# A decode block on one Trainium2 core: W_gate loaded in three pieces by partitions, x in three loads instead of five

## The chip, the core and the metric

The kernel runs on one core of a Trainium2 chip. A core has a matrix engine (TensorE, PE), a vector engine (VectorE, DVE), a scalar engine (ScalarE, ACT), GpSimd (POOL), a queue engine that only issues and waits (SyncE, SP), and sixteen DMA engines that bring data from the device's memory into the 128 partitions of the on-chip memory. The metric is the device time of one execution in microseconds (us); lower is better. A load here means one DMA instruction; a load over 128 partitions is cut into rows, one to a partition, and the rows are dealt out to the DMA engines.

## What is computed

One decode step of a transformer layer for two sequences (B = 2, one new token each): layer norm, attention over a cache of 8192 positions with 32 heads of 128, a residual, a second layer norm, and a gated feed-forward with a rectified gate.

```python
# x (2,1,512); k_cache, v_cache (2,32,8192,128); wq (512,4096); wo (4096,512)
# W_gate, W_up (512,1376); W_down (1376,512); all bfloat16
q = layernorm(x) @ wq                      # 32 heads of 128
p = softmax(q . k_cache * 128 ** -0.5)
h = x + (p . v_cache) @ wo
n = layernorm(h)
gate = n @ W_gate
gate = gate * (gate > 0)
out = h + (gate * (n @ W_up)) @ W_down
```

The two caches are 268 MB of the 281 MB that are read, so the work is mostly a stream of cache tiles through the core.

## The kernel before

All of the order is written by hand: the body stands under `tc.manual_schedule()`, and each engine executes its instructions in the order of the text.

The on-chip memory holds three large buffers, `bufs[0]` to `bufs[2]`, of 64 KB in each partition. A tile of K or V covers four heads of one sequence (8 MB) and fills one buffer. A "step" is one such group of heads: 15 full steps and, for the last four heads, two half steps of two heads each (`steps`, `Q` is the last full step). K of step i lies in buffer 2i mod 3 and V in 2i+1 mod 3, so that one of the three is always being filled. Within a step VectorE multiplies the K tile by the query (L375) and adds up along the head dimension (L393, L395), while TensorE and ScalarE take a share of the positions by transposing them (L349, L350, L340). Then come the softmax's exponentials (L415) and the product with V on TensorE (L446).

The loads are issued by two queues. ScalarE's queue issues only x: five loads at L190, into `xr`, two rows of `bufs[2]`. SP's queue issues everything else, in the order of the text: W_q (L193), K and V of the first step (L165, `load_tile`), then one cache tile each time a buffer comes free, and in the last stage W_o in six pieces (L567, L589, L590), W_gate and W_up (L612), three pieces of the last 96 rows of W_down (L616) and four loads with the rest of it (L621). A load waits on its issuing queue until the buffer that it writes has been read. The tile framework numbers the loads of both queues round eight semaphores, so that a load also waits until the load eight before it has landed.

At the front TensorE transposes x (L238), VectorE and ScalarE norm it (`ln_cols`, L172 to L185), TensorE multiplies it with W_q (L252), and the queries are spread over the partitions (L259 to L276). This work needs x and W_q, and runs while the first K tile is still on its way. At the end the attention output is multiplied by W_o (`attend_set`, `attend`), normed, and goes through W_gate and W_up (`through`, L686) and W_down (`down`, L719). W_gate and W_up lie behind each other in `bufs[2]` as `wgu`: partition p holds rows 4p to 4p+3 of the matrix, 11,008 bytes for each of the two. The copies at L734 and L735 and the store at L736 close the kernel.

Of the kernel before, what the change touches and what calls it, by code (L numbers as in the profile page):

```python
# [13 lines left out]
def _free(t, offset, dims):  # L14

    return bass.AP(tensor=t.tensor, offset=t.offset + offset, ap=[t.ap[0]] + [list(d) for d in dims])


def _dram(t, offset, dims):
    return bass.AP(tensor=t.tensor, offset=t.offset + offset, ap=[list(d) for d in dims])  # L20
# [3 lines left out]
def kernel(  # L24
# [13 lines left out]
    nc = tc.nc  # L38
    P = nc.NUM_PARTITIONS
# [3 lines left out]
    F = B_W_gate.shape[1]  # L43
    KC = D // P
# [81 lines left out]
    wgu = bufs[2][:, HALF:HALF + 2 * KC * F].rearrange("p (k c f) -> p k c f", k=2, c=KC)  # L126
# [59 lines left out]

    with tc.manual_schedule():

        for b, k, n in ((0, 0, 2), (0, 2, 2), (1, 0, 2), (1, 2, 1), (1, 3, 1)):
            nc.scalar.dma_start(  # L190
                out=xr[b:b + 1, k * P:(k + n) * P], in_=_dram(A_x, b * D + k * P, [[D, 1], [1, n * P]]),
            )
# [9 lines left out]
            out=nscale, in_=nscale, compare_op=ALU.not_equal, fill=-SCALE,  # L202
# [5 lines left out]
            out=ident_f, in_=ident_f, compare_op=ALU.not_equal, fill=1.0,  # L208
# [4 lines left out]
            out=sel, in_=sel, compare_op=ALU.not_equal, fill=1.0,  # L213
# [9 lines left out]
            out=pick, in_=pick, compare_op=ALU.not_equal, fill=1.0,  # L223
# [24 lines left out]
        for g0 in range(0, NQ, 4):  # L248
            for n0 in range(NH * g0 * Dh, NH * (g0 + 4) * Dh, 4 * Dh):
                q_ps = ps2.tile([B, 4 * Dh], f32, tag="o")  # L250
                for c in range(KC):
                    nc.tensor.matmul(  # L252
                        out=q_ps, lhsT=xn[:, c, :], rhs=wq_sb[:, c, n0:n0 + 4 * Dh], start=(c == 0), stop=(c == KC - 1),
                    )
                nc.vector.tensor_copy(qrow[:, n0:n0 + 4 * Dh], q_ps)
            for b in range(B):
                r_ps = ps2.tile([P, 4, Dh], f32, tag="tp")
                for j in range(NH):
                    nc.tensor.matmul(  # L259
                        out=r_ps[j * (P // NH):(j + 1) * (P // NH)], lhsT=sel[:, b, 0:P // NH],  # L260
# [5 lines left out]
        for j in range(2):  # L266
            nc.tensor.matmul(
                out=r_ps[j * (P // 2):(j + 1) * (P // 2)], lhsT=sel[:, B - 1, :],
# [102 lines left out]
        def products(s, t0=0, t1=None):  # L371

            n = (s.nv if t1 is None else t1) - t0
            kv = _free(s.kt, t0 * Dh, [[Dh, n], [1, Dh]])
            nc.vector.tensor_tensor(out=kv, in0=kv, in1=_free(s.qr, 0, [[0, n], [1, Dh]]), op=ALU.mult)  # L375
# [211 lines left out]
        for k in range(1, len(SETS)):  # L587
# [3 lines left out]
            out=wo[:, (HM + 1) * D:Hq * D], in_=_dram(A_wo, (HM + 1) * Dh * D, [[P // 4 * D, 4], [D, P // 4], [1, D]]),  # L591
# [16 lines left out]
        scores_pe(p1, lambda: next(turns)())  # L608
        act_sums(p1)
        products(p1, 48)  # L610
        for w, src in ((0, B_W_gate), (1, B_W_up)):
            nc.sync.dma_start(  # L612
                out=wgu[:, w].rearrange("p c f -> p (c f)"), in_=_dram(src, 0, [[KC * F, P], [1, KC * F]]),
            )
        for q0 in range(AGAIN, P, AGAIN):
            nc.sync.dma_start(  # L616
                out=wd_sb[q0:q0 + AGAIN, FC - 1, :], in_=_dram(B_W_down, (F - P + q0) * D, [[D, AGAIN], [1, D]]),
            )
        for f0, n in FSETS[:-1]:
# [10 lines left out]
            out=z2_ps, lhsT=ones, rhs=_free(zc, ((B - 1) * NQ + groups[Q][1]) * NH, [[1, nb]]), start=True, stop=True,  # L630
# [63 lines left out]
        for c in range(KC):  # L694
            nc.tensor.transpose(hT_ps[:, c, :], hb[:, c].rearrange("p k b -> p (k b)"), ident)
        nc.scalar.activation(
            out=hrow.rearrange("q (p c) -> q p c", c=KC), in_=hT_ps.rearrange("q c p -> q p c"), func=ACT.Copy,
# [9 lines left out]
            out=gate, in0=g_ps, scalar=0.0, in1=_free(rvar, 0, [[0, FC], [1, B]]), op0=ALU.max, op1=ALU.mult,  # L707
# [16 lines left out]
        for t, (part, _, _) in zip(u_ps, parts):  # L724
            through(t, 1, part)
            f = slice(part[0], part[-1] + 1)
# [40 lines left out]
```

## Time and profile before

| | us |
|---|---|
| median of 3 runs | 659.67 (659.04 to 659.94) |
| profiled execution | 659.39 |
| its span in the profile | 657.5 |
| VectorE busy | 558.1 (85% of the span) |
| TensorE busy (matmul) | 352.1 (54%) |
| ScalarE busy | 123.6 (19%) |
| bytes read | 281.05 MB, 427 GB/s over the span |

"Busy" is the time in which an engine executes; the span runs from the first to the last event of the profile, and what the profiled execution took beyond it lies before and after the span. The page divides the span into 40 slices and gives for each engine the busy share in tenths (9 is 90% or more). The chain of waits is followed back from the last instruction: at each step to whatever released it. In its lines, and in those of the timeline, the columns are the start in us, the duration in us, and what it was; a name such as `tile L375` is the written tile and the line in the program, and SPq and ACTq are queue instructions, such as the issue of a load. A line of the waits reads: engine, line, what was waited for, then the total in us, the number of waits and the longest. A load's time in the chain is from its issue to its last completion, with the time that it stands behind earlier loads in it. For each load the trace also records the completions, one for each DMA engine that took part, and every single packet with its start, its duration and its size.

### The profile page before, as it was taken

The numbers are of one execution on the slowest core, as the hardware profiler recorded it, in microseconds if no ns is written. First come the engines' busy times: TensorE is split into PE (matmuls) and PEld (weight loads), VectorE is DVE, ScalarE is ACT, GpSimd is POOL, SyncE is SP. The second block draws the span as 40 slices with busy tenths as digits, with TensorE's granted clock in tenths as the row PEclk, the third lists the DMA queues.
The fourth block names the chain that finished last, engine by engine and source line by source line (L and its number), as shares of the span: only waits on it lengthen the run. The fifth ranks groups of instructions, "written<-read, shape, count | busy, mean of one in ns | idle before, by whom it ended". The sixth has DMA issues, their size and how long they took to land.

```text
span 657.5 us, 5117 instructions
## 1 busy us (share of the span) xinstructions
PE 352.1 (54%) x2118; PEld 158.9 (24%) x2118; DVE 558.1 (85%) x252; ACT 123.6 (19%) x337; POOL 24.1 (4%) x36
## 2 busy tenths in 40 slices
PE   0730934809175380926539092552918458291997
PEld 0310311304022130312204031220403224030456
DVE  0599697988979799897979989796997969999982
ACT  0230030200203020030301103030210304201870
POOL 3080000000000000000000000000000000000020
PEclk9975775958778596877959687695968869686895
DMA  9999999999999999999999999999999999999997
GB/s 383 447 444 447 387 440 443 447 399 444 439 443 436 419 436 435 439 439 436 423 443 424 439 440 427 447 416 443 439 423 440 423 443 436 423 444 413 425 425 291
DMA packets 6948, 281.37 MB, mean 428 GB/s; under 512 B 809, under 2 KB 1422, under 8 KB 1934
## 3 DMA queue, kind: packets, MB, share of 16 engines
q1 hardware_dynamic: 6916, 281.06, 99.1%
q8 instruction: 16, 0.26, 0.1%
q14 instruction: 6, 0.05, 0.0%
q10 hardware_dynamic: 10, 0.00, 0.0%
HBM read 281.05 MB, written 0.00 MB: 427 GB/s over the span
## 4 chain that ended last, share of the span: by engine, by line
DVE 42%; DMA 37%; PE 18%; ACT 1%; issue 1%; ACTq 0%; SPq 0%; DVEq 0%
DMA tile<-in_A_k_cache_dram 30%; DVE tile L375 19%; DVE tile L393 18%; PE pv_ps L446 16%; DMA tile<-in_A_wo_dram 4%; DVE scol L395 2%; DMA tile<-in_A_x_dram 2%; DMA tile<-in_B_W_down_dram 1%; PE q_ps L252 1%; DVE pgq L420 1%; ACT ecol L415 1%; DVE pm L399 1%; DVE qrep L395 0%; DVE pm L410 0%; DVE hmax L412 0%
## 5 line engine op out<-in xcount | busy, mean ns | idle before, releaser
L446 PE MATMUL pv_ps<-tile,pgq 128*16 128x512 bf16 x960 | 244.3, 421 | 235.8 <-DVE pgq L420 223.2
L375 DVE TENSOR_TENSOR tile<-tile,qrep 128x29696 bf16<-128x29696 bf16 (+3 forms) x16 | 232.4, 14524 | 44.9 <-DMA tile<-in_A_k_cache_dram 44.9
L393 DVE TENSOR_TENSOR tile<-tile 128x14848 bf16<-128x14848 bf16 (+7 forms) x68 | 236.4, 3477 | 2.2
L446 PEld LDWEIGHTS <-pgq 128*16 128x16 bf16 x960 | 91.6, 97 | 378.1 <-DVE pgq L420 234.5
L451 ACT ACTIVATE pv<-pv_ps 16x512 f32<-16x512 f32 (+1 forms) x16 | 9.4, 589 | 243.7 <-PE pv_ps L446 243.6
L350 ACT ACTIVATE tile<-t_ps 128x1024 bf16<-128x1024 bf16 x53 | 52.6, 1022 | 12.6 <-PE t_ps L349 12.1
L415 ACT ACTIVATE ecol<-scol,nmax 128x256 bf16<-128x256 f32 x14 | 7.1, 508 | 196.1 <-DVE nmax L414 196.1
L340 PE MATMUL row_ps<-tile,qz 128*24 128x512 bf16 (+1 forms) x98 | 30.1, 389 | 18.0 <-ACT tile L350 17.9
L349 PE MATMUL t_ps<-ident,tile 128*128 128x128 bf16 x424 | 32.3, 229 | 13.0 <-DMA tile<-in_A_k_cache_dram 13.0
L349 PEld LDWEIGHTS <-tile 128*128 128x128 bf16 x424 | 25.8, 103 | 28.1 <-issue 14.2
L395 DVE TENSOR_REDUCE scol<-tile 128x232 f32<-128x1856 bf16 (+1 forms) x14 | 28.9, 2067 | 0.5
L641 POOL TENSOR_TENSOR tile<-ident 6x2 bf16<-6x2 bf16 x1 | 2.1, 2147 | 583.5 <-ACT tile L381 583.5
L420 DVE TENSOR_TENSOR pgq<-ecol,ownb 128x1024 bf16<-128x1024 bf16 x15 | 10.4, 692 | 10.3 <-ACT ecol L415 10.3
L381 ACT ACTIVATE tile<-tile 128x128 bf16<-128x128 bf16 x60 | 17.6, 293 | 1.9 <-DVE tile L375 1.9
L281 POOL COPY qzp<-qTs 128x4 bf16<-128x4 bf16 x1 | 15.0, 14982 | 26.1 <-DVE qTs L276 26.1
L375 DVE TENSOR_TENSOR tile<-tile,qpair 128x4096 bf16<-128x4096 bf16 (+3 forms) x4 | 15.5, 3883 | 0.0
L340 PEld LDWEIGHTS <-qz 128*24 128x24 bf16 (+1 forms) x98 | 7.9, 92 | 27.6 <-issue 22.7
L239 DVE CAST xc<-x_ps 128x8 f32<-128x8 bf16 x1 | 0.2, 167 | 15.5 <-PE x_ps L238 15.5
L367 ACT ACTIVATE scol<-sc_ps 32x24 f32<-32x24 f32 (+1 forms) x56 | 11.7, 209 | 7.7 <-PE sc_ps L362 7.2
L362 PE MATMUL sc_ps<-ident_f,tile 24*128 24x24 f32 (+2 forms) x68 | 7.2, 220 | 11.1 <-ACT tile L358 11.1
L358 ACT ACTIVATE tile<-row_ps 24x512 f32<-24x512 f32 (+2 forms) x17 | 10.0, 586 | 13.5 <-PE row_ps L340 13.5
L381 ACT ACTIVATION_READ_ACCUMULATOR tile<-tile 128x1 f32 x60 | 11.2, 186 | 0.0
(133 smaller groups left out, 143.8 us busy)
## 6 DMA issues: line engine op xcount, KB each, us to landing
tile<-in_A_k_cache_dram SPq DMA_DIRECT2D x2, 4096.0 KB
tile<-in_A_v_cache_dram SPq DMA_DIRECT2D x2, 4096.0 KB, 19.6
tile<-in_A_wq_dram SPq DMA_DIRECT2D x1, 4096.0 KB, 12.2
tile<-in_A_wo_dram SPq DMA_DIRECT2D x1, 2048.0 KB
tile<-in_B_W_gate_dram SPq DMA_DIRECT2D x1, 1376.0 KB, 22.8
tile<-in_B_W_up_dram SPq DMA_DIRECT2D x1, 1376.0 KB
tile<-in_A_wo_dram SPq DMA_DIRECT2D x1, 1024.0 KB, 23.8
tile<-in_B_W_down_dram SPq DMA_DIRECT2D x1, 640.0 KB
```

Source lines behind the costliest of these rows:

```text
L281: nc.gpsimd.tensor_copy(qzp[:, :, 6:8], qTs[:, B - 1, Hq - NH:Hq].rearrange("p (k j) -> p k j", j=2),)
L340: nc.tensor.matmul(out=row_ps, lhsT=z, rhs=s.kt[:, (nv + c0 + k) * Dh:(nv + c0 + k + 4) * Dh], start=(u == 0), stop=(u == U - 1),)
L349: nc.tensor.transpose(t_ps[:, k, :], s.kt[:, t * Dh:(t + 1) * Dh], ident)
L350: nc.scalar.activation(out=s.kt[:, (nv + c0) * Dh:(nv + c0 + TPC) * Dh], in_=t_ps.rearrange("p t s -> p (t s)"), func=ACT.Copy,)
L367: nc.scalar.activation(out=scols[s.i][r, nv:s.nt].rearrange("p (u t) -> p t u", t=4), in_=sc_ps[r, :, :, j], func=ACT.Copy,)
L375: nc.vector.tensor_tensor(out=kv, in0=kv, in1=_free(s.qr, 0, [[0, n], [1, Dh]]), op=ALU.mult)
L381: nc.scalar.activation(out=kv, in_=kv, func=ACT.Copy, accum_out=scols[s.i][:, t:t + 1])
L393: nc.vector.tensor_tensor(out=lo, in0=lo, in1=hi, op=ALU.add)
L395: nc.vector.tensor_reduce(out=scol[:, s.na:s.nv], in_=_free(s.kt, s.na * Dh, [[Dh, s.nv - s.na], [1, 8]]), axis=AXIS.X, op=ALU.add,)
L415: nc.scalar.activation(out=ecol, in_=scols[s.i], func=ACT.Exp, scale=SCALE, bias=nmax, accum_out=zs[:, s.b, s.g:s.g + 1],)
L420: nc.vector.tensor_tensor(out=s.pg, in0=_free(ecol, 0, [[VG, s.nt // VG], [0, NH], [1, VG]]), in1=_free(ownb, 0, [[0, s.nt // VG], [VG, NH ...
L446: nc.tensor.matmul(out=pv_ps[s.i][r, :], lhsT=s.pg[:, u].rearrange("p j t -> p (j t)"), rhs=s.vt[:, u * VG * Dh:(u + 1) * VG * Dh], start= ...
```

## The change

x comes by three loads: the first sequence's 512 values by one, the second's by two of 256. W_gate, before one load over 128 partitions, comes by three, over partitions 0 to 7, 8 to 15 and 16 to 127; W_up stays one load. The number of loads in the whole program stays the same (two fewer on ScalarE's queue, two more on SP's).

```diff
-        for b, k, n in ((0, 0, 2), (0, 2, 2), (1, 0, 2), (1, 2, 1), (1, 3, 1)):
+        for b, k, n in ((0, 0, 4), (1, 0, 2), (1, 2, 2)):
             nc.scalar.dma_start(
                 out=xr[b:b + 1, k * P:(k + n) * P], in_=_dram(A_x, b * D + k * P, [[D, 1], [1, n * P]]),
             )
...
-        for w, src in ((0, B_W_gate), (1, B_W_up)):
-            nc.sync.dma_start(
-                out=wgu[:, w].rearrange("p c f -> p (c f)"), in_=_dram(src, 0, [[KC * F, P], [1, KC * F]]),
-            )
+        for w, src, cuts in ((0, B_W_gate, (0, 8, 16, P)), (1, B_W_up, (0, P))):
+            for q0, q1 in zip(cuts, cuts[1:]):
+                nc.sync.dma_start(
+                    out=wgu[q0:q1, w].rearrange("p c f -> p (c f)"),
+                    in_=_dram(src, q0 * KC * F, [[KC * F, q1 - q0], [1, KC * F]]),
+                )
```

## The prediction

> **What bounds the kernel now.** First the page: its second part (the span in 40 slices) and its fourth (the chain that ended last).
>
> ```profile
> span 657.5 us, 5117 instructions
> ...
> DVE  0599697988979799897979989796997969999982
> DMA  9999999999999999999999999999999999999997
> ...
> HBM read 281.05 MB, written 0.00 MB: 427 GB/s over the span
> ```
>
> The DMA row has no gap in it until the last slice; VectorE, the busiest engine, has. The span is the time that 281 MB take. The trace keeps every DMA packet, and I followed the sixteen DMA engines packet by packet: from 1.8 us until 654 us each packet starts within some nanoseconds of the end of the one before it on its engine. A change pays only if it shortens or rebalances what those sixteen carry.
>
> Second, the chain in order of time, at its two ends:
>
> ```profile
> 2.11 12.96 DMA tile<-in_A_x_dram
> 15.07 0.14 issue
> 15.20 0.28 PE x_ps L238 x4
> ...
> 30.63 0.31 PE r_ps L267 x2
> 30.96 41.50 DMA tile<-in_A_k_cache_dram
> 72.48 15.64 DVE tile L375
> ...
> 618.99 24.67 DMA tile<-in_A_wo_dram
> ...
> 644.18 9.77 DMA tile<-in_B_W_down_dram
> 653.94 0.04 issue
> 653.99 0.60 PE d_ps L719 x15
> 654.61 0.33 PE d_ps L719 x4
> 654.97 0.27 ACT tile L735
> ```
>
> At the front x lands at 15.07, and the second K tile's load is issued at 30.96. Its 41.50 us are not its own: an 8 MB load takes 19.3 us, so it stood behind two others. At the back W_down's last pieces land at 653.94 and, by the landing records, 654.57; four matmuls, the copies and the store follow: 2.9 us of tail. The profiled execution took 659.39 us: 657.5 of span and 1.9 around it. The median of the runs, 659.67, is 0.28 more, and I add that to every time below.
>
> Third, the waits of SP's queue, which issues all loads but x:
>
> ```profile
> SPq L616 <- DMA tile<-in_A_v_cache_dram: 9.3, 1, 9.3
> SPq L612 <- DMA tile<-in_A_wo_dram: 4.5, 1, 4.5
> SPq L612 <- DMA tile<-in_A_v_cache_dram: 4.4, 1, 4.4
> SPq L621 <- DMA tile<-in_B_W_gate_dram: 2.6, 1, 2.6
> ```
>
> A load waits until the one issued eight loads before it has landed (there are eight load semaphores, taken in turn): L612 for V's half tile, L621 for W_gate.
>
> The landing records also show what no page prints: the sixteen engines don't finish together. Each load has sixteen completions, and W_gate's are (us):
>
> ```
> 644.59 644.62 644.65 644.65 644.77 645.14 646.10 646.12
> 646.35 646.36 647.37 647.48 647.54 647.58 647.59 647.63
> ```
>
> Six engines are done by 645.1, six only from 647.4 on. The lead grows over the run by steps of about 1.6 us, each on one engine, just after one of sixteen 16 KB packets of the instruction queue (q8, at 36.8, 94.8, 155.4 us and so on, 0.88 to 1.0 us each); they go round eight engines, twice. W_down's last load ends at 651.57 on the first engine and 654.57 on the last: the slow engines set the end.
>
> **The change, part by part.**
>
> *x.* Its completions are at 1.96, 7.74, 10.19, 12.62 and 15.07 us: after the first, each load costs one turn between W_q's packets for its data and one for its semaphore, 2.44 us. With three the last lands at 10.19, 4.88 us earlier, whatever the bytes (512 or 1,024 B are one packet of some 25 ns). The queries follow, 3.5 us from x to the normed row, at 13.7; W_q's last completion, 12.96, is just ahead. What hides the 4.88 us is the K tile behind it: K's first tile completes at 32.26, and VectorE's first product starts at 32.41. So at most 0.15 us there, and then nothing: the K load issued at 30.96 could be issued at 26 and would still stand behind V, which lands at 53.1. Were that cover gone, x would be worth up to 4.88. I take 0.
>
> *W_gate, how it is spread.* The engines that a load uses show in its completions: one row of x, one; the two rows of the output, two; 32 rows of W_down, sixteen, with two rows each in the packets; 128 rows, sixteen with eight. I take eight rows as eight engines with one row each, and 112 as sixteen with seven. Of 128 rows, eight engines then carry nine and eight carry seven, where each had eight. A row of 11,008 B takes 413 ns in the packets. So eight engines end 0.41 us later than before and eight 0.41 earlier. The sum has two ends: -0.41 if all slow engines are among the relieved, +0.41 if one slow engine is among the loaded; the packets do not name their engine, and I could follow the engine that carries x only up to a three-way tie at 92.4 us. One slow engine among the loaded is enough, so I take +0.41.
>
> [...]
>
> *W_gate, how it is issued.* SP issues two loads more, 0.33 us each, in time in which it waits anyway. By the eight-loads rule W_gate's three pieces wait for V's half tile (624.8), for the first part of W_o (629.7, where W_up was issued) and for V's last half tile (639.3). W_up now waits for the second part of W_o, 641.8; W_down's pieces queue behind it: 643.1, 643.7, 644.0, 644.3, then each W_gate piece in turn, the last at about 648 instead of 647.6. Do the engines run dry? The earliest engine finishes W_o at 641.32. The piece issued at 639.3 needs some 1.0 us to its first packet (W_q: issued at 0.74, first packet at 1.78), so 1.0 us is left. W_up, issued at 641.8, arrives at 642.9 and is needed at 644.2 (641.32 and seven rows). W_down's last piece is needed at 651.3. No gap: 0. The matmuls that read W_gate start at 648.24, waiting for VectorE; W_gate now lands at about 648.0, still ahead.
>
> *Sum:* 0 + 0.41 + 0 = +0.41: 659.39 + 0.41 = 659.80, and with 0.28 660.1 us.
>
> **The rivals.**
>
> *Eight adjacent rows share a way into memory (slower).* The place is the two eight-row loads: eight engines write eight neighbouring partitions at once. If these can take no more than one or two engines' pace, the rows queue. Between none and all eight in series (8 x 0.413 = 3.30 us instead of 0.41) lie 0 and 2.9 us a load, 0 and 5.8 for both, on top of the 0.41. For it: no load of the trace has put so many bytes into so few partitions. Against it: the rows of the 32-row loads, two to an engine, take 46 ns per 1,024 B, exactly as in the 128-row loads; but those are too short to fill anything. Halfway, 2.9 us: 659.39 + 0.41 + 2.9 + 0.28 = 663.0 us. It decides from 0.9 us for the pair on a slow engine; if the eight are the six early ones and two more, their 3 us lead hides most of it.
>
> [...]
>
> *x was the bound after all (faster).* The chain does run through x, and VectorE's first product starts 0.15 us after K's tile. Up to 4.88 us: 654.8. Against it: the DMA engines have no gap between 1.8 and 654 us, and their bytes stay.
>
> *It does not do what it says.* If an eight-row load were cut over all sixteen engines, nothing moves but x: 659.7.
>
> **How the numbers follow.** The forecast (every row at its engine's own pace, one row more or less per engine) has 0.43, the shared way 0.41, x 0.10, no effect 0.06. The forecast's own range is 659.1 to 660.4: -0.41 to +0.41 around 659.67 with some scatter (the runs lie 0.9 us apart). A difference under 0.2%, 1.3 us, is about what a measurement of this kernel can tell from no change. Within it lie the forecast and no effect: 0.49. Slower by more is the shared way: 0.41; faster is x: 0.10. The range reaches from 659.0 to the shared way's 663.0; outside are x and the upper part of the shared way, together some 0.2.
>
> **What would show it.** x's last completion near 10.2 us and VectorE's first product still at 32.3 to 32.4: x is hidden. The 11,008 B packets: eight engines with nine, eight with seven. If those packets stay at 413 ns and W_down's last completion lies within 0.5 us of 654.57, the forecast's price is right; if the packets of the first two loads are stretched to two or four times 413 ns, the shared way is there. W_down's completions should lie closer together if the loaded engines are the early ones, and wider apart if they are the late ones. The prediction is wrong if the end moves by more than 1.3 us, or if a gap opens on an engine between 640 and 650 us because a load was issued too late.

## The result and the profile after

| | us |
|---|---|
| median after, 6 runs | 664.89 (664.13 to 665.96) |
| median before beside it, 6 runs | 659.53 (659.04 to 659.94) |
| ratio | 1.0083 [1.007, 1.0096] |
| profiled execution after, its span | 665.37, 663.6 |

The change makes the kernel 5.4 us slower, and the span of the profiled execution is 6.1 us longer. The page of the changed kernel, in the same lines as before:

```profile
span 663.6 us, 5115 instructions
...
DMA  9999999999999999999999999999999999999996
GB/s 379 442 439 442 442 436 403 431 443 432 443 438 436 411 436 438 431 435 436 438 427 432 438 443 419 435 439 435 431 435 436 423 436 438 438 406 437 438 349 196
...
HBM read 281.05 MB, written 0.00 MB: 424 GB/s over the span
```

The bytes are the same, and the DMA row still has no gap until the last slice. What is new stands in the GB/s row, last slice but one: 349 after 438 in the slice ahead of it. The engines are as busy there as ever and bring less. The same row of the kernel before has no such drop, 425 in both slices:

```profile
GB/s 383 447 444 447 387 440 443 447 399 444 439 443 436 419 436 435 439 439 436 423 443 424 439 440 427 447 416 443 439 423 440 423 443 436 423 444 413 425 425 291
```

The chain of waits after (start, duration, what), at its two ends, and then its last pieces:

```profile
1.53 8.68 DMA tile<-in_A_x_dram
13.70 5.84 PE q_ps L252 x16
...
26.71 45.49 DMA tile<-in_A_k_cache_dram
72.31 15.64 DVE tile L375
...
624.99 22.45 DMA tile<-in_B_W_gate_dram
647.49 12.51 DMA tile<-in_B_W_down_dram
```

```profile
660.04 0.59 PE d_ps L721 x10
...
660.67 0.33 PE d_ps L721 x4
```

x has landed at 10.21 us (1.53 + 8.68), and the matmuls of the queries run from 13.70. The second K tile's load is issued at 26.71, 4.25 us earlier than before, but now takes 45.49 us instead of 41.50: both end at about 72.2 to 72.5, and VectorE's second step begins at 72.31 where it was 72.48. V's first half tile lands at 624.92 (before: 624.77) and its last half tile at 639.41 (before: 639.28). So all but 0.1 us of the loss lies after 639 us. W_down's last completion is at 660.63; it was 654.57.

The next view divides the last stage into stretches. Its columns: from and to, length, the busy time (and count) of PE, PEld, VectorE, ScalarE and POOL, then the granted clock of TensorE, the DMA engines' busy share and GB/s. Before:

```profile
642.00:646.00 4.00, 3.68 (x109) 3.59 (x108) 0.78 (x5) 0.00 (x0) 0.00 (x0) 0.50 1.04 432
646.00:650.00 4.00, 3.23 (x77) 3.07 (x75) 1.33 (x9) 0.00 (x0) 0.00 (x0) 0.50 1.00 401
650.00:654.00 4.00, 3.61 (x82) 2.97 (x83) 1.02 (x6) 0.59 (x1) 0.00 (x0) 0.50 0.70 267
```

After:

```profile
642.00:646.00 4.00, 3.65 (x108) 3.56 (x107) 0.80 (x5) 0.00 (x0) 0.00 (x0) 0.50 1.12 250
646.00:650.00 4.00, 1.70 (x32) 1.46 (x29) 1.33 (x9) 0.00 (x0) 0.00 (x0) 0.50 1.01 224
650.00:654.00 4.00, 0.00 (x0) 0.03 (x1) 0.00 (x0) 0.00 (x0) 0.00 (x0) 0.50 0.93 265
```

The share in the last column but one is near 1 in both; the last column falls from 432 and 401 to 250 and 224 GB/s. The packets say how: the 11,008 B packets, one row of W_gate or W_up each, took 413 ns before (median; mean 419.5) and take 729 ns after (mean 695, longest 1,082). Their sum grew from 107.4 to 177.9 us, 70.5 us over sixteen engines or 4.4 us for each. Packets of other loads that are in flight at the same time are stretched too: 31 of W_o's last 128 packets of 4,096 B take up to 324 ns instead of 159. The sixteen completions of W_down's last load come 5.2 us later in the mean; the last of them, 1.3 us behind that mean before, is now 2.2 us behind it, which makes up the 6.1 us. PE pays for it: from 646 to 650 us it is busy for 1.70 us instead of 3.23.

SP's waits after:

```profile
SPq L613 <- DMA tile<-in_A_v_cache_dram: 14.1, 2, 9.4
...
SPq L623 <- DMA tile<-in_B_W_gate_dram: 5.8, 2, 5.6
SPq L618 <- DMA tile<-in_A_wo_dram: 2.8, 3, 2.0
```

W_down's last load waits 5.6 us (before: 2.6) for W_gate's third piece, whose last completion is at 653.87. This is a consequence and not the cause: no engine falls idle for it, since sixteen packets or more are under way at every full microsecond from 640 to 656.

### The profile page after: what moved, and what is told of

Read it like the earlier page. It is cut to its first block, busy times and chain, and to the rows that moved or that the text cites. A ratio compares the mean times of both kernels' runs of the same rounds, so it can differ in the third digit from the quotient of the medians.

```text
span 663.6 us, 5115 instructions
## 1 busy us (share of the span) xinstructions
PE 353.8 (53%) x2118; PEld 159.7 (24%) x2118; DVE 558.2 (84%) x252; ACT 123.7 (19%) x337; POOL 9.1 (1%) x36
## 4 chain that ended last, share of the span: by engine, by line
DVE 42%; DMA 40%; PE 17%; ACT 1%; issue 1%; ACTq 0%; DVEq 0%; SPq 0%
DMA tile<-in_A_k_cache_dram 30%; DVE tile L375 19%; DVE tile L393 18%; PE pv_ps L446 15%; DMA tile<-in_B_W_gate_dram 3%; DMA tile<-in_A_v_cache_dram 3%; DVE scol L395 2%; DMA tile<-in_B_W_down_dram 2%; PE q_ps L252 1%; DMA tile<-in_A_x_dram 1%; DVE pgq L420 1%; ACT ecol L415 1%; DVE pm L399 0%; DVE qrep L395 0%; DVE pm L410 0%
## 5 line engine op out<-in xcount | busy, mean ns | idle before, releaser
L362 PEld LDWEIGHTS sc_ps<-ident_f,tile 24*128 24x128 f32 (+2 forms) x68 | 5.5, 136 | 19.4 <-ACT tile L358 19.4
L252 PE MATMUL q_ps<-tile,xn 128*2 128x512 bf16 x32 | 9.5, 460 | 1.0 <-DVE xn L185 1.0
```

What stands on the lines that cost most here:

```text
L252: nc.tensor.matmul(out=q_ps, lhsT=xn[:, c, :], rhs=wq_sb[:, c, n0:n0 + 4 * Dh], start=(c == 0), stop=(c == KC - 1),)
L362: nc.tensor.transpose(sc_ps[:, t].rearrange("p u j -> p (u j)"), rows[:, t * P:(t + 1) * P], ident_f[0:nh * U, 0:nh * U],)
```

## The experiments

Each kernel was timed beside the kernel before on the same chip; ratios are to that, with 95% intervals. All of them have x in three loads, so that only the last stage differs between them. The diffs are against the changed kernel where its line with the cuts stands with a minus, against the experiment before in one section that says so, and otherwise against the kernel before, without the part on x; `...` marks lines left out. "Packets" are those of 11,008 B.

### x alone

```diff
-        for w, src, cuts in ((0, B_W_gate, (0, 8, 16, P)), (1, B_W_up, (0, P))):
+        for w, src in ((0, B_W_gate), (1, B_W_up)):
...
```

> x in three loads, W_gate in one as before. Every theory that puts the loss into W_gate's pieces expects the time of the kernel before, 659.5 us within 0.5, with x's last completion at 10.2 us and VectorE's first product still at 32.3 to 32.4. Were x to blame in part, the time would lie between 659.5 and 664.9.

659.47 us, ratio 1.0004 [0.9995, 1.0013]; packets 413 ns; span 657.5 us, as before. x costs and gives nothing.

### The eight-row loads alone

W_gate stays one load; two loads of eight rows are added, into partitions 0 to 7 and 8 to 15 of a part of `bufs[2]` that is not read.

```diff
+        for q0 in (0, 8):
+            nc.sync.dma_start(
+                out=bufs[2][q0:q0 + 8, HALF + 2 * KC * F:TILE],
+                in_=_dram(B_W_gate, q0 * KC * F, [[KC * F, 8], [1, TILE - HALF - 2 * KC * F]]),
+            )
```

> W_gate in one load of 128 partitions, and ahead of it two loads of eight partitions (10,752 B a row) into unused memory: the eight-row loads alone, at the cost of 16 rows more to read. Theory A (the load of 112 partitions is what halves the pace: its rows, seven to an engine, take the engines off the ways into memory that they have to themselves) expects only the extra bytes: two rows on eight engines, 0.8 us at most, 659.5 to 660.4. Theory B (the rows of an eight-row load queue behind each other in a few partitions, as in the rival of the prediction) expects most of the loss: 662 to 666 us, with row packets stretched well over 413 ns around the two loads only.

661.12 us, ratio 1.0034 [1.0021, 1.0046]: between the two expectations, about 2 us. Packets 442 ns (mean 491, longest 1,152). The stretches of the last stage:

```profile
642.00:646.00 4.00, 3.69 (x109) 3.60 (x109) 0.76 (x5) 0.00 (x0) 0.00 (x0) 0.50 1.04 297
646.00:650.00 4.00, 1.52 (x30) 1.34 (x28) 1.33 (x9) 0.00 (x0) 0.00 (x0) 0.50 0.99 394
```

The dip lasts while these two loads are in flight, and from 646 us the pace is nearly back. The sixteen added packets, 404 ns each in the last eight-row run below, take 602 ns in the mean and 1,115 at most. So there is a cost at the eight-row loads, but less than half of what has to be explained.

### The 112-row load alone

W_gate by one load into partitions 16 to 127; rows of partitions 0 to 15 are left out.

```diff
-        for w, src, cuts in ((0, B_W_gate, (0, 8, 16, P)), (1, B_W_up, (0, P))):
+        for w, src, cuts in ((0, B_W_gate, (16, P)), (1, B_W_up, (0, P))):
```

> W_gate by one load of 112 partitions; rows of partitions 0 to 15 of W_gate are left out. Theory A expects the slow stretch without the eight-row loads: the packets of 11,008 B at 700 ns or more, and a time of 662 to 664.5 us. Theory B expects a load like any other with one row less for each engine: packets of 413 ns, 659.1 us.

664.96 us, ratio 1.0087 [1.0072, 1.0102], with 16 rows fewer to bring. Packets 780 ns (mean 750):

```profile
642.00:646.00 4.00, 3.69 (x109) 3.60 (x109) 0.76 (x5) 0.00 (x0) 0.00 (x0) 0.50 1.08 201
646.00:650.00 4.00, 1.99 (x30) 1.57 (x28) 0.79 (x6) 0.00 (x0) 0.00 (x0) 0.50 1.01 207
```

Half pace for eight microseconds and more. The large piece, which the prediction had at its engines' own pace, costs all of it by itself.

### Two halves of 64 rows

```diff
-        for w, src, cuts in ((0, B_W_gate, (0, 8, 16, P)), (1, B_W_up, (0, P))):
+        for w, src, cuts in ((0, B_W_gate, (0, 64, P)), (1, B_W_up, (0, P))):
```

> W_gate in two loads of 64 partitions, four rows to an engine, no engine with more than another. Theory A in the form 'an engine has its own way only to its share of a 128-partition load, and any other dealing makes engines meet' expects half pace here too: packets of some 800 ns, and 662 to 665 us. If only an uneven dealing (seven rows) is the trouble, or the unequal number of rows per engine, 659.5 us. A theory of the source side (the order in which the device's memory is read) has no reason for a loss where each engine reads four whole rows: 659.5 us.

664.78 us, ratio 1.0084 [1.0069, 1.0099], packets 752 ns:

```profile
642.00:646.00 4.00, 3.99 (x122) 3.99 (x122) 0.55 (x3) 0.00 (x0) 0.00 (x0) 0.50 1.05 233
646.00:650.00 4.00, 1.19 (x16) 0.93 (x13) 1.33 (x9) 0.00 (x0) 0.00 (x0) 0.50 1.04 230
```

The loss needs no eight-row piece and no seven rows to an engine; two halves, four rows to an engine, are enough.

### The same 64 rows, in other partitions

Two kernels load 64 rows of W_gate and leave the others out: into partitions 32 to 95, and into partitions 0 to 63.

```diff
-        for w, src, cuts in ((0, B_W_gate, (0, 8, 16, P)), (1, B_W_up, (0, P))):
+        for w, src, cuts in ((0, B_W_gate, (32, 96)), (1, B_W_up, (0, P))):
```

```diff
-        for w, src, cuts in ((0, B_W_gate, (0, 8, 16, P)), (1, B_W_up, (0, P))):
+        for w, src, cuts in ((0, B_W_gate, (0, 64)), (1, B_W_up, (0, P))):
```

> W_gate by one load of 64 rows into partitions 32 to 95; the rows of the other 64 partitions are left out. Both this and its twin deal four rows to an engine from the same kind of source rows; only the partitions that they go to differ. Theory C (the engines meet at the partitions: which ones a load covers decides) expects this load at full pace: packets of 413 ns, 1.65 us less than with all 128 rows, 657.5 to 658.0 us. Theory D (any load that is not dealt as the 128-partition loads are is slow, wherever it goes) and a theory of the source side expect it as slow as its twin. [...]

> The twin: one load of 64 rows into partitions 0 to 63, the rest of W_gate left out. Theory C and theory D both expect it slow: packets of 11,008 B at 700 ns or more around it, and a time well above the twin's, 659.5 to 662.5 us. If it were as fast as the twin, two half loads in a row would be needed for the loss that the two loads of 64 partitions showed.

Partitions 32 to 95: 658.35 us, ratio 0.9984 [0.9975, 0.9993], a little above what was expected; packets 413 ns, none over 475.

```profile
642.00:646.00 4.00, 3.75 (x112) 3.66 (x112) 0.76 (x4) 0.00 (x0) 0.00 (x0) 0.50 1.05 434
```

Partitions 0 to 63: 661.84 us, ratio 1.0043 [1.0029, 1.0056]; packets 750 ns.

```profile
642.00:646.00 4.00, 3.73 (x110) 3.64 (x110) 0.76 (x4) 0.00 (x0) 0.00 (x0) 0.50 1.08 230
646.00:650.00 4.00, 1.65 (x29) 1.39 (x27) 1.33 (x9) 0.00 (x0) 0.00 (x0) 0.50 0.95 225
```

Same rows in number, same bytes, same sixteen completions: 434 against 230 GB/s. The number of rows does not decide. That partitions 32 to 95 would run at full pace was the author's guess: no run before gives a reason for it, and these two show the figures and not the reason. What differs is which partitions the load covers, and with them which rows it reads, since row p always goes to partition p; rows 32 to 63 are in both loads. No run sent the same rows to other partitions, so that a cause on the reading side is made unlikely, by these shared rows and by the next run, and not excluded.

### All rows, even partitions and odd partitions

In place of the changed kernel's pieces W_gate comes by two loads; W_up stays one load.

```diff
...
+        for q0 in range(2):
             nc.sync.dma_start(
+                out=wgu[q0:P:2, 0].rearrange("p c f -> p (c f)"),
+                in_=_dram(B_W_gate, q0 * KC * F, [[2 * KC * F, P // 2], [1, KC * F]]),
             )
...
```

> All of W_gate by two loads of 64 rows, one into the even partitions, one into the odd ones: no load covers fewer than two partitions of any four neighbours. If only the count of partitions that a load covers in each neighbourhood matters, this is near full pace, 659.5 to 660.5 us. [...]

659.31 us, ratio 1.0001 [0.9992, 1.001]; packets 413 ns (mean 416.9):

```profile
642.00:646.00 4.00, 3.49 (x101) 3.34 (x101) 0.92 (x5) 0.00 (x0) 0.00 (x0) 0.50 1.02 422
646.00:650.00 4.00, 3.28 (x79) 3.15 (x78) 1.34 (x9) 0.00 (x0) 0.00 (x0) 0.50 1.01 413
```

W_gate in two loads of 64 rows costs nothing by even and odd partitions (659.31 us), where the halves 0 to 63 and 64 to 127 cost 5.5 us (664.78). Which engine wrote which row was not seen, so that this run does not decide whether that matters.

### W_down's last rows in one load

The kernel before has 32-row loads of its own, into partitions 32 to 63, 64 to 95 and 96 to 127. Here one load over 128 partitions replaces them, and the clearing of the first 32 moves behind it.

```diff
-        for q0 in range(AGAIN, P, AGAIN):
-            nc.sync.dma_start(
-                out=wd_sb[q0:q0 + AGAIN, FC - 1, :], in_=_dram(B_W_down, (F - P + q0) * D, [[D, AGAIN], [1, D]]),
-            )
+        nc.sync.dma_start(out=wd_sb[:, FC - 1, :], in_=_dram(B_W_down, (F - P) * D, [[D, P], [1, D]]))
...
```

> x in three loads, W_gate plain, and the last 128 rows of W_down by one load of 128 partitions instead of three loads of 32; the 32 rows that are there twice are set to zero behind the load instead of ahead of it. If loads that don't cover all partitions slow their neighbours, then so do these three, in the kernel before too: its packets between 648.8 and 650.2 us are stretched from 413 to 450 to 500 ns. Then this kernel shows no packets over 420 ns there (but for those next to an instruction packet) and gains 0.2 to 0.6 us: 658.9 to 659.3 us where the kernel before has 659.5. If the stretch has another cause, it stays, and the time is the same or 0.1 us longer (32 rows more to read).

659.33 us, ratio 1.0001 [0.9992, 1.0009]: no gain that can be measured; the 0.2 to 0.6 us that were expected did not show. In the packets the effect is complete: of W_down's 128 packets of 5,120 B, 27 took over 10 ns more than 196 ns in the trace of before, up to 247, and now all 128 take 196 ns; of those of 3,072 B 25 were stretched as much, now none. W_down's last completion is at 654.24 us; with x alone changed it was 654.39.

### The eight-row loads, one row to a neighbourhood

The two added eight-row loads again, the same bytes, to every fourth partition; the diffs here are against the kernel with the eight-row loads alone, and the second against the first.

```diff
-        for q0 in (0, 8):
+        for q0 in (0, 64):
             nc.sync.dma_start(
-                out=bufs[2][q0:q0 + 8, HALF + 2 * KC * F:TILE],
-                in_=_dram(B_W_gate, q0 * KC * F, [[KC * F, 8], [1, TILE - HALF - 2 * KC * F]]),
+                out=bufs[2][q0:q0 + 32:4, HALF + 2 * KC * F:TILE],
+                in_=_dram(B_W_gate, q0 * KC * F, [[4 * KC * F, 8], [1, TILE - HALF - 2 * KC * F]]),
             )
```

> [...] Rival (a load that only eight engines carry is itself what costs): as with rows 0 to 15, 661.1, with about 297 GB/s in 642 to 646 us.

660.61 us, ratio 1.0019 [1.001, 1.0028]: better than rows 0 to 15 (661.12), and still 1.3 us above the kernel before (659.32), where the sixteen added rows of 404 ns are by estimate 0.40 us if sixteen engines share them and 0.81 if eight do. The packets are 413 ns in the median but 452 in the mean:

```profile
642.00:646.00 4.00, 3.83 (x117) 3.83 (x118) 0.71 (x4) 0.00 (x0) 0.00 (x0) 0.50 1.04 389
646.00:650.00 4.00, 2.60 (x65) 2.45 (x62) 1.33 (x9) 0.00 (x0) 0.00 (x0) 0.50 1.03 406
```

From 641.3 to 642.5 us no packet takes over 422 ns; 51 of those that start before 648.2 us take over 430, 48 of them between 642.5 and 645 us. Both added loads are in flight then (completions from 641.32 to 644.70 and from 641.96 to 645.47), so that this run alone does not say which of them does it; of their own sixteen packets twelve take 404 ns, and those that are stretched are W_gate's and W_up's. So rows spread over every fourth partition are not enough. The next run moves the second load alone, from partitions 64, 68, ..., 92 to 1, 5, ..., 29.

```diff
-        for q0 in (0, 64):
+        for q0 in (0, 1):
```

> [...]

659.85 us, ratio 1.0006 [0.9997, 1.0015]. Two of the 207 packets before 648.2 us are over 430 ns, and all sixteen added packets take 404 ns:

```profile
642.00:646.00 4.00, 3.60 (x106) 3.51 (x106) 0.85 (x5) 0.00 (x0) 0.00 (x0) 0.50 1.04 428
646.00:650.00 4.00, 3.23 (x79) 3.07 (x78) 1.34 (x9) 0.00 (x0) 0.00 (x0) 0.50 1.00 414
```

Back to 428 GB/s, though the sixteen rows lie closer together than in the run before, all in partitions 0 to 29. Two loads of eight rows run at full pace here, so that the rival of the run before, that such loads cost by themselves, falls; and how evenly the loads cover the partitions does not decide alone. The two runs differ in where the second load's eight rows go, and in 389 against 428 GB/s; which engine wrote where was not seen, and why the place matters is not shown.

### 96 rows, by one load and by three

One kernel loads 96 rows of W_gate by one load into partitions 32 to 127, the other by three loads into partitions 1, 5, 9 and so on, 2, 6, 10 and 3, 7, 11. The remaining 32 rows are left out in each; the second diff shows the three loads that stand in place of W_gate's pieces. The "theory of cover" is the author's, that a load which covers the partitions evenly costs its bytes and no more.

```diff
-        for w, src, cuts in ((0, B_W_gate, (0, 8, 16, P)), (1, B_W_up, (0, P))):
+        for w, src, cuts in ((0, B_W_gate, (32, P)), (1, B_W_up, (0, P))):
```

```diff
...
+        for q0 in range(1, 4):
             nc.sync.dma_start(
+                out=wgu[q0:P:4, 0].rearrange("p c f -> p (c f)"),
+                in_=_dram(B_W_gate, q0 * KC * F, [[4 * KC * F, P // 4], [1, KC * F]]),
             )
...
```

> W_gate by one load of 96 rows into partitions 32 to 127, rows 0 to 31 left out; x by three loads. [...] If any uneven cover brings everything down to half pace, as the 112-row load did: packets near 750 ns, 200 to 250 GB/s in 642 to 650 us, 662.5 to 664.5. If unevenness were not it: 413 ns and 658.5.

> [...] Three loads, so that W_up and W_down wait on the queue exactly as in the changed kernel. Theory of cover: packets at 413 ns, above 400 GB/s until the bytes run out, and 32 rows fewer (0.35 MB, 0.8 us): 658.4 to 659.2. Rival (three loads in place of one, their issue or the order of the waits behind them, bear part of the cost): over 660 or a gap in the packets between 640 and 650 us.

By one load: 663.82 us, ratio 1.0064 [1.0051, 1.0077], packets 767 ns (mean 699).

```profile
642.00:646.00 4.00, 3.69 (x109) 3.61 (x109) 0.76 (x4) 0.00 (x0) 0.00 (x0) 0.50 1.08 236
646.00:650.00 4.00, 1.78 (x30) 1.50 (x28) 1.33 (x9) 0.00 (x0) 0.00 (x0) 0.50 0.99 213
```

By three: 658.56 us, ratio 0.9987 [0.9978, 0.9996], packets 413 ns (mean 421).

```profile
642.00:646.00 4.00, 4.00 (x124) 4.00 (x125) 0.45 (x3) 0.00 (x0) 0.00 (x0) 0.50 1.05 434
646.00:650.00 4.00, 3.29 (x63) 2.90 (x60) 1.34 (x9) 0.25 (x1) 0.00 (x0) 0.50 1.00 382
```

The same bytes differ by 5.3 us, and the three loads, with the queue behind them as in the changed kernel, are the faster. The count of loads, their issue and their waits cost nothing that can be measured.

## Why the prediction was wrong

**The bound.** Right: the sixteen DMA engines carry the end. Before, all of them are busy until 651.57 us, when the first has brought its share (at 653 us eight are still at work, so that "no gap between 1.8 and 654 us" holds for the slow ones alone). But "busy" was read as "at full pace".

**x, 0.** Right, at the place and in the numbers named: last completion at 10.21 us, K's first tile at 32.25, and alone it makes 1.0004. (The packet of 1,024 B took 44 ns and not some 25; nothing hangs on it.)

**W_gate, how it is spread: the step that failed.** The counts of completions were right: the first two pieces have eight each, the third has sixteen. That both eight-row loads fall on the same eight engines, on which the +0.41 rests, no run shows: the packets don't name their engine. The step then went on: "A row of 11,008 B takes 413 ns in the packets. So eight engines end 0.41 us later than before and eight 0.41 earlier." That price did not hold. Of the 256 rows of W_gate and W_up 249 took over 430 ns, 695 in the mean, and where the sum had +0.41 the change cost 5.4 us. Most of it was not the dealing of one row more or less but the pace of all engines (in the profiled execution 5.2 of 6.1 us by the mean of the last completions), and the third piece alone, which the step had at seven rows of 413 ns to an engine, is enough for it (664.96). In the runs the price of a row goes with which partitions the loads in flight cover: 413 ns beside a load over 32 to 95, 750 beside one over 0 to 63. Why the partitions matter is not shown. In one run with eight-row loads the price holds: with the two added ones at 0, 4, ..., 28 and 1, 5, ..., 29 the packets stay at 413 and 404 ns, and the time is 659.85 where the kernel before has 659.39 beside it; sixteen rows of 404 ns over sixteen engines are 0.40.

**W_gate, how it is issued, 0.** Right: no engine ran dry, and the three loads of 32 rows show it without the stretching. W_gate's landing, forecast for 648.0 us and ahead of its matmuls, came at 653.87, and they started at 654.00 instead of 648.24; the end still hangs on W_down, which landed later.

**The rival of the shared way.** Its idea, that rows slow each other by where they are written, is what the runs point to; its place and the size it was given (663.0) were not right. Its place was "the two eight-row loads"; these alone make some 2 us, while the 112-row load alone makes 664.96. The rival asked how many rows of one load meet in a few partitions and did not ask it of the large piece. And it counted only the rows of that load in series, where the runs show the loads in flight beside it slowed as well. The upper bound worked out for it, 5.8 us on top of 0.41, would have held the result, but by luck, since most of the loss comes from the piece that it does not count; the range stopped at half of it.

**The argument against it** was that W_down's 32-row loads take 46 ns a packet, as in plain loads, "but those are too short to fill anything". The sign was one view further, in the packets beside them: 27 of 128 packets of 5,120 B were stretched by up to 26% (247 against 196 ns), and with those loads replaced none is. A price taken from the suspect's own packets misses what it does to its neighbours'.

**What remains open.** The packets don't name their engine, so which rows of the 112 each engine gets was not seen. Nor does a run show why that load comes with half the pace (201 GB/s), and the loads of all even and all odd partitions (422 GB/s) and the three of 32 rows (434 GB/s) with full pace. And no run sent the same rows to other partitions. It is also open why the two eight-row pieces add nothing to what the 112-row piece costs alone. No version that loads all rows came out faster than the kernel before by more than a measurement can tell.

## What to carry to other kernels

Where the DMA engines set the time, ask of every load that is not over all 128 partitions which partitions it covers, and read its effect off the packets of all loads in flight, since a busy share near 1 says nothing of the pace (1.00 at 401 GB/s before, 1.01 at 224 after, from 646 to 650 us). If rows have to be split over several loads, split them by stride (every second or fourth partition) and not by ranges: two loads of 64 rows cost nothing by even and odd partitions and 5.5 us as halves. A stride alone is no warrant: the two eight-row loads to every fourth partition cost 1.3 us from 0 and 64, bytes included, and 0.5 from 0 and 1.

## What the runs showed of the chip

From 642 to 646 us, where the kernel before brings 432 GB/s with packets of 413 ns, the kernel with one load of W_gate over partitions 0 to 63 brings 230 GB/s with packets of 750 ns, and the one with a load over 32 to 95 434 GB/s with 413 ns. With a load over 16 to 127 the pace was 201 GB/s. The strided loads of 64 and 32 rows run at full pace (422 and 434 GB/s).

The same eight-row loads give 297, 389 and 428 GB/s by where they go (partitions 0 to 15; every fourth from 0 and from 64; every fourth from 0 and from 1). Which engine gets which row, and why the place matters, no run here shows.
